# Moving a unit's y product behind the next unit's scores, in one PSUM tile of four banks

## The chip, the core and the metric

The kernel runs on one core of one Trainium2 chip. Its time is the device time of one execution in microseconds (us). Of the kernel before, three runs took 572.52, 573.49 and 574.24 us, so the median is 573.49 us. The profile shows one execution of 573.5 us, whose span from the first to the last instruction is 571.7 us. The other 1.8 us lie around the span.

## The reference

A gated linear attention is followed by two mixtures of matrix products, all in float32. For each of 32 rows (batch x head), the sequence of 768 positions is cut into chunks:

```python
L = np.exp(cum[:, :, :, None] - cum[:, :, None, :]) * causal
CB = np.einsum('bhin,bhjn->bhij', Cc, Bc)
y = np.einsum('bhij,bhjd->bhid', CB * L, xc) + np.einsum('bhin,bhnd->bhid', Cc, state) * decay_to_i
state = decay_full * state + np.sum(Bx, axis=2)
...
a = x @ w1; b = x @ w2; x = (a * b @ w3) @ w_out          # 3072 tokens, 256 -> 1024 -> 256
h = np.maximum(x @ w_in, 0.0); out = (h * h) @ w_out2       # 256 -> 2048 -> 256
```

## The kernel before, in words

The tokens are worked in eight blocks of 384 tokens (here blocks 0 to 7, so that the third block is block 2). A large product is three passes of TensorE over split operands (high x high, high x low, low x high, `mm3`, line 187), each a 128x128 by 128x384 matmul. w3 and w_out are multiplied together once, into `wc`. A block has two phases. Phase a has eight slots (m = 0 to 7): twelve matmuls for a and b into two PSUM tiles `w`, a copy on ScalarE (ACT, `asb`), a product on VectorE (DVE, `pr`), a cast on ACT (`s3h`) and a remainder on DVE (`s3l`, line 537), and three slots later six matmuls that sum x2 into two tiles `acc`. Phase h has sixteen slots (slots 8 to 23 of the block): six matmuls into a tile `w`, the relu on ACT (`r`), its square on GpSimd (POOL, `q`), the square's cast on ACT (`s3h`), the remainder on DVE (`s3l`, line 577), and three slots later six matmuls into two `acc` tiles. At the start of phase h three products h(0), h(1) and h(2) are begun together, so three tiles are open at once.

The attention is cut into 16 units; a block needs the y of two of them. A unit has these steps. Four scans on DVE make the decays (`la`, line 347). `u_lw` (DVE, line 359) ends them. `u_bt` (line 251), `u_bd` (line 365) and `u_w2` (line 376) on POOL prepare weights. `u_cb` makes four score tiles on TensorE (line 427), and `u_gain` the state sums (line 385). `u_m` multiplies scores by decays on DVE (four times, line 438), `u_state` carries the state (DVE, line 398), `u_carry` copies it into the weights of y (ACT, four copies, line 409), `u_y` makes y on TensorE (line 445), and `u_x` and `u_xl` (lines 465 and 472) write it, split, as the x of its block. A unit's loads are `la` (line 227), `xa`, and for every second unit `ct` and `bs`.

The first two blocks and units 0 to 5 run in an order written out by hand (`ORDER`). From block 2 on the order is that of the loops `ph_a` and `ph_h`, and the steps of units 6 to 15 are put into slots by the table `AT` (lines 103 to 106 and 787 to 789): unit u is worked in block u // 2 - 1, in the slots that its row names. `run_fill` calls a slot's steps before the slot's remainder on DVE, so they stand in each engine's queue ahead of it.

PSUM has eight banks: three tiles `w`, two `acc`, two `cb`, one `yu`. A unit's scores take both `cb`, one `w` and `yu`; `yu` also holds the state sums, and later y, over the place of the fourth scores.

Of the kernel before, what the change touches and what calls it, by code (L numbers as in the profile page):

```python
# [5 lines left out]
F32 = mybir.dt.float32  # L6
F32R = mybir.dt.float32r
# [15 lines left out]
HC = HG * NCH

FBS = [TB] * 8
NF = len(FBS)
F0 = [sum(FBS[:f]) for f in range(NF)]
FB = max(FBS)
M1 = FF1 // 128
M2 = FF2 // 128  # L30
KD = DM // 128
# [13 lines left out]
EARLY = 6  # L45
PLANNED = 2
# [53 lines left out]
}  # L100


AT = [
    [0, 1, 3, 5, 5, 6, 7, 7, 7, 8, 9, 9, 11, 13, 14, 14, 14],
    [6, 6, 13, 13, 14, 16, 18, 18, 19, 19, 19, 20, 20, 22, 22, 22, 23],
]


class Plan:
# [25 lines left out]
def mixer_kernel(ctx, tc, a, bct, xb, cst, *rest):  # L135
# [15 lines left out]
    nc = tc.nc  # L151
# [6 lines left out]
    at = ctx.enter_context(tc.tile_pool(name="at", bufs=2))  # L158
    sb = ctx.enter_context(tc.tile_pool(name="sb", bufs=2))
    late = ctx.enter_context(tc.tile_pool(name="late", bufs=1))  # L160
    ps_w = ctx.enter_context(tc.tile_pool(name="ps_w", bufs=3, space=PSUM))
    ps_acc = ctx.enter_context(tc.tile_pool(name="ps_acc", bufs=2, space=PSUM))
    ps_cb = ctx.enter_context(tc.tile_pool(name="ps_cb", bufs=2, space=PSUM))
    ps_yu = ctx.enter_context(tc.tile_pool(name="ps_yu", bufs=1, space=PSUM))

    cs = const.tile([TA, TB], F32, name="cs")
    sel = const.tile([128, 2 * H], F32R, name="sel")
# [13 lines left out]
    def f32(t):  # L181
        return t.bitcast(F32)
# [42 lines left out]
    def load_la(u):  # L225
        t = at.tile([TA, LA], F32, tag="la", name="la")
        nc.sync.dma_start(out=t, in_=az[u:u + 1, :].to_broadcast([TA, LA]))
        raw.setdefault(u, {})["la"] = t

    def load_xa(u):  # L230
        t = at.tile([TA, HC * D + HC * N], F32, tag="xa", name="xa")
        nc.sync.dma_start(out=t[0:T, :], in_=xb[u])  # L232
        raw.setdefault(u, {})["xa"] = t

    def load_ct(j, h):

# [141 lines left out]
    def u_gain(u):  # L378

        d = un[u]  # L380
        b = bd[u % 2]
        for c in range(NCH):
            for h in range(HG):
                i = h * NCH + c
                nc.tensor.matmul(  # L385
                    d["yu"][32 * h:32 * h + 32, TB + c * D:TB + (c + 1) * D],
                    lhsT=b[:, i * N:i * N + 2 * N],
                    rhs=d["xa"][0:T, i * D:(i + 1) * D],
                    start=True, stop=True,
                )  # L390

    def u_state(u):

        d = un[u]
        s = st[u % 2]
        c0 = NCH * ((u // 2) % 2)
        for c in range(NCH):
            nc.vector.scalar_tensor_tensor(
                s[:, c0 + c + 1, :], s[:, c0 + c, :], w2s[u % 2][:, c:c + 1],
                d["yu"][:, TB + c * D:TB + (c + 1) * D], ALU.mult, ALU.add,  # L400
            )

    def u_carry(u):

        d = un[u]
        s = st[u % 2]
        c0 = NCH * ((u // 2) % 2)
        for h in range(HG):
            nc.scalar.copy(
                d["xa"][T:TA, h * NCH * D:(h + 1) * NCH * D].rearrange("p (c d) -> p c d", d=D),  # L410
                s[32 * h:32 * h + N, c0:c0 + NCH, :],
            )

    def u_cb(u):


        d = un[u]
        hs = range(HG)
        for h in range(2):
            d["cb", h] = ps_cb.tile([128, TB], F32, tag="cb", name="cb")  # L420
        d["cb", 2] = ps_w.tile([128, 512], F32, tag="w", name="cbw")[:, 0:TB]
        d["yu"] = ps_yu.tile([128, 512], F32, tag="yu", name="yu")
        d["cb", 3] = d["yu"][:, 0:TB]
        for c in range(NCH):
            for h in hs:
                r = slice(32 * h, 32 * h + N)
                nc.tensor.matmul(  # L427
                    d["cb", h][0:TA, c * T:(c + 1) * T],
                    lhsT=bt[u % 2][r, c, :],
                    rhs=d["ct"][r, c * T:(c + 1) * T],  # L430
                    start=True, stop=True,
                )

    def u_m(u, h):

        d = un[u]
        s = d["la"][:, h * LH:h * LH + TB]
        nc.vector.tensor_tensor(s, d.pop(("cb", h))[0:TA, :], s, op=ALU.mult)

    def u_y(u):  # L440
        d = un[u]
        for c in range(NCH):
            for h in range(HG):
                i = h * NCH + c
                nc.tensor.matmul(  # L445
                    d["yu"][32 * h:32 * h + 32, c * T:(c + 1) * T],
                    lhsT=d["xa"][:, i * D:(i + 1) * D],
                    rhs=d["la"][:, h * LH + c * T:h * LH + (c + 1) * T],
                    start=True, stop=True,
                )  # L450

    def u_x(u):

        d = un[u]
        d["x"] = []
        j, g = divmod(u, 2)
        at0 = j * TB
        while at0 < (j + 1) * TB:
            f = max(f for f in range(NF) if F0[f] <= at0)
            end = min(F0[f] + FBS[f], (j + 1) * TB)  # L460
            if f not in xt:
                xt[f] = [sb.tile([128, KD, FB], F32R, tag=f"xt{p}", name=f"xt{p}", bufs=2) for p in "hl"]
            hi, lo = (t[:, g, at0 - F0[f]:end - F0[f]] for t in xt[f])
            src = d["yu"][:, at0 - j * TB:end - j * TB]
            nc.scalar.copy(hi, src)
            d["x"].append((lo, src, hi))
            at0 = end

    def u_xl(u):
        raw.pop(u)  # L470
        for lo, src, hi in un.pop(u)["x"]:
            nc.vector.tensor_tensor(lo, src, f32(hi), op=ALU.subtract)

    def u_loads(u):
        if u < NU:
            load_la(u)
            load_xa(u)
            if u % 2:
                for h in range(HG):
                    load_ct(u // 2, h)  # L480
                    load_bt(u // 2, h)

    def unit_steps(u):
        return [
            *(lambda h=h: u_decay(u, h) for h in range(HG)),
            lambda: (u_lw(u), u_bt(u)),
            lambda: (u_bd(u), u_w2(u)),
            lambda: (u_cb(u), u_gain(u)),
            lambda: u_m(u, 2),
            lambda: u_m(u, 3),  # L490
            lambda: u_state(u),
            lambda: u_m(u, 0),
            lambda: u_m(u, 1),
            lambda: u_carry(u),
            lambda: u_y(u),
            lambda: u_loads(u + 2),
            lambda: u_x(u),
            lambda: u_xl(u),
        ]

    pt = {}
    x2 = {}
    qt = {}
    acc = {}
    hp = {}
# [46 lines left out]
    def ff_h1(f, m, k, which=(0, 1, 2)):  # L552
        x = x2[f]
        if m not in hp:
            hp[m] = ps_w.tile([128, 512], F32, tag="w", name="pw")[:, 0:FBS[f]]
        mm3(hp[m], [t[:, k, m * 128:(m + 1) * 128] for t in wi], [t[:, k, :] for t in x], k == 0, k == KD - 1, which)

    hr = {}
# [217 lines left out]
    plan.run(ORDER)  # L776


    fill = {}
    at_slot = [PLANNED * (M1 + M2)]  # L780

# [2 lines left out]
            f()  # L784
        at_slot[0] += 1

    for u in range(EARLY, NU):
        for i, f in zip(AT[u % 2], unit_steps(u)):
            fill.setdefault((u // 2 - 1) * (M1 + M2) + i, []).append(f)

    def ph_a(f, tail):
        for m in range(M1):
# [111 lines left out]
```

## Time and profile before

| what | value |
|---|---|
| median of three runs | 573.49 us |
| profiled execution | 573.5 us, span 571.7 us |
| TensorE busy | 561.6 us, 98% of the span |
| weight loads busy (PEld) | 538.4 us, 94% |
| DVE, ACT, POOL busy | 330.8, 287.8, 134.7 us |
| granted TensorE clock | full in all 40 slices of the span |
| chain that ended last | TensorE 91%, DMA 6% |

A row of a timeline gives the start, the duration, the engine, the line, the operation, what it writes and reads, how many such instructions are merged, and in brackets how long the engine had been idle and what released it. Starts of successive rows tell what an engine's rate is; the duration of a matmul includes its way through the array, so it overlaps the next. For a merged row on DVE, ACT or POOL the duration runs from the first start to the last end.

### The profile page before, as it was taken

How to read it: one execution, taken by the hardware profiler on the slowest of the kernel's cores; microseconds unless marked ns; L12 is line 12 of the kernel's file. 1: busy time of each engine (PE TensorE's matmuls, PEld its weight loads, DVE VectorE, ACT ScalarE, POOL GpSimd, SP SyncE). 2: the span in 40 equal slices, each digit the busy share in tenths (PEclk: the TensorE clock that was granted, in tenths of full speed). 3: DMA queues.
4: the chain of work that ended last, by engine and by line, in shares of the span. 5: the costliest groups of instructions: out<-in, count | busy, mean ns of one | idle time of the engine just before them, and what ended most of it. 6: DMA issues, size and time to landing. Idle time of an engine off the chain costs nothing.

```text
span 571.7 us, 11523 instructions
## 1 busy us (share of the span) xinstructions
PE 561.6 (98%) x4518; PEld 538.4 (94%) x4518; DVE 330.8 (58%) x625; ACT 287.8 (50%) x611; POOL 134.7 (24%) x210
## 2 busy tenths in 40 slices
PE   8988999999999999999999999999999999999997
PEld 5866999999999999999999999999999999999997
DVE  6879899993655456435554556535554556433421
ACT  2688777853446326443455326443454326443443
POOL 3133214010000014421153014421253014410342
PEclk9999999999999999999999999999999999999999
DMA  8998967100121001040021302040022200000000
GB/s 224 385 338 277 292 197 206 50 1 29 50 58 49 29 1 57 16 97 29 1 70 57 69 2 64 8 99 28 1 70 69 59 1 1 1 2 29 0 1 28
DMA packets 17182, 43.53 MB, mean 76 GB/s; under 512 B 2744, under 2 KB 7080, under 8 KB 17128
## 3 DMA queue, kind: packets, MB, share of 16 engines
q1 hardware_dynamic: 16840, 42.58, 24.5%
q8 instruction: 35, 0.57, 0.4%
q10 hardware_dynamic: 288, 0.22, 0.2%
q14 instruction: 19, 0.16, 0.1%
HBM read 39.55 MB, written 3.25 MB: 75 GB/s over the span
## 4 chain that ended last, share of the span: by engine, by line
PE 91%; DMA 6%; SPq 1%; ACT 1%; DVE 1%; POOL 0%; issue 0%; ACTq 0%; POOLq 0%
PE pw L187 48%; PE acc L187 36%; DMA rawl<-in_w3t 3%; PE acc L616 2%; PE cb L427 2%; PE yu L445 2%; DMA rawe<-in_w3t 2%; DMA ct<-in_bct 1%; PE yu L385 1%; SPq L247 0%; ACT wch L630 0%; SPq L277 0%; DVE la L347 0%; ACT rawe L294 0%; SPq L232 0%
## 5 line engine op out<-in xcount | busy, mean ns | idle before, releaser
L577 DVE TENSOR_TENSOR s3l<-q,s3h 128x384 fp32r<-128x384 f32 x128 | 75.6, 598 | 102.9 <-POOL q L570 88.3
L187 PE MATMUL acc<-s3h,wo 128*128 128x384 f32 x512 | 132.4, 340 | 0.0
L570 POOL TENSOR_TENSOR q<-r 128x384 f32<-128x384 f32 x97 | 84.2, 870 | 185.9 <-ACT r L562 167.8
L562 ACT ACTIVATE r<-pw 128x384 f32<-128x384 f32 x128 | 62.3, 488 | 89.1 <-PE pw L187 85.5
L187 PEld LDWEIGHTS acc<-s3h,wo 128*128 128x128 f32 x512 | 91.9, 188 | 1.8
L187 PE MATMUL pw<-x2h,wih 128*128 128x384 f32 x256 | 86.6, 338 | 0.0
L187 PE MATMUL pw<-x2h,wil 128*128 128x384 f32 x256 | 86.4, 338 | 0.0
L187 PE MATMUL acc<-s3l,wo 128*128 128x384 f32 x256 | 86.1, 336 | 0.0
L187 PE MATMUL pw<-x2l,wih 128*128 128x384 f32 x256 | 84.9, 339 | 0.0
L524 DVE TENSOR_TENSOR pr<-pw,asb 128x384 f32<-128x384 f32 x64 | 35.6, 557 | 66.3 <-PE pw L187 60.3
L574 ACT ACTIVATE s3h<-r 128x384 fp32r<-128x384 f32 x128 | 67.0, 525 | 11.3 <-PE acc L187 7.7
L534 ACT CAST s3h<-pr 128x384 fp32r<-128x384 f32 x55 | 28.3, 514 | 65.4 <-DVE pr L524 61.8
L520 ACT COPY asb<-pw 128x384 f32<-128x384 f32 x64 | 30.6, 479 | 46.4 <-PE pw L187 45.4
L347 DVE TENSOR_TENSOR_SCAN la<-la,cs 112x384 f32<-112x384 f32 x48 | 49.0, 1042 | 0.0
L187 PEld LDWEIGHTS pw<-x2h,wih 128*128 128x128 f32 x256 | 48.1, 188 | 0.3
L187 PEld LDWEIGHTS acc<-s3l,wo 128*128 128x128 f32 x256 | 48.0, 188 | 0.3
L187 PEld LDWEIGHTS pw<-x2l,wih 128*128 128x128 f32 x256 | 47.9, 188 | 0.3 <-DVE x2l L550 0.3
L187 PEld LDWEIGHTS pw<-x2h,wil 128*128 128x128 f32 x256 | 48.1, 188 | 0.0
L365 POOL TENSOR_TENSOR bd<-xa,la 96x256 f32<-96x256 f32 x16 | 11.5, 720 | 142.6 <-DVE la L359 133.0
L187 PE MATMUL pw<-xth,w1h 128*128 128x384 f32 x128 | 43.6, 341 | 0.0
L187 PE MATMUL pw<-xth,w2h 128*128 128x384 f32 x128 | 43.6, 340 | 0.0
L187 PE MATMUL pw<-xth,w1l 128*128 128x384 f32 x128 | 43.3, 338 | 0.0
(109 smaller groups left out, 1040.3 us busy)
## 6 DMA issues: line engine op xcount, KB each, us to landing
la<-az SPq DMA_DIRECT2D x12, 679.0 KB, 4.6
xa<-in_xb SPq DMA_DIRECT2D x16, 288.0 KB, 5.6
rawe<-in_w3t SPq DMA_DIRECT2D x9, 512.0 KB, 9.3
rawl<-in_wo SPq DMA_DIRECT2D x7, 512.0 KB, 7.3
rawl<-in_w3t SPq DMA_DIRECT2D x7, 512.0 KB, 9.1
out_t<-o SPq DMA_DIRECT2D x16, 192.0 KB, 2.0
rawe<-in_wo SPq DMA_DIRECT2D x5, 512.0 KB, 7.6
rawl<-in_w SPq DMA_DIRECT2D x5, 512.0 KB, 9.1
```

The lines of the kernel that those rows point to most:

```text
L187: nc.tensor.matmul(ps, lhsT=w[i == 1], rhs=x[i == 2], start=first and i == 0, stop=last and i == 2)
L347: nc.vector.tensor_tensor_scan(la[:, 0:TB], src[:, 0:TB], cs, 0.0, ALU.mult, ALU.add)
L365: nc.gpsimd.tensor_tensor(bd[u % 2][:, 0:HC * N].rearrange("p (h c n) -> p h c n", h=HG, n=N), d["xa"][0:T, HC * D:].rearrange("p (h c n) ...
L427: nc.tensor.matmul(d["cb", h][0:TA, c * T:(c + 1) * T], lhsT=bt[u % 2][r, c, :], rhs=d["ct"][r, c * T:(c + 1) * T], start=True, stop=True,)
L445: nc.tensor.matmul(d["yu"][32 * h:32 * h + 32, c * T:(c + 1) * T], lhsT=d["xa"][:, i * D:(i + 1) * D], rhs=d["la"][:, h * LH + c * T:h * L ...
L520: nc.scalar.copy(ab[m], ab.pop((m, 0)))
L524: nc.vector.tensor_tensor(pr, ab.pop((m, 1)), ab[m], op=ALU.mult)
L534: (nc.scalar.copy if eng == "ACT" else on[eng].tensor_copy)(pt[f, m][0], ab[m])
L562: nc.scalar.activation(hr[m], hp.pop(m), AF.Relu)
L570: on[eng].tensor_tensor(q, hr[m], hr[m], op=ALU.mult)
L574: nc.scalar.activation(qt[f, m][0], hr[m], AF.Square)
L577: nc.vector.tensor_tensor(qt[f, m][1], hr.pop((m, 0)), f32(qt[f, m][0]), op=ALU.subtract)
```

## The change

From unit 6 on a unit's scores, state sums and the y of the unit before it are issued together (`u_turn`): scores of unit u, state sums of unit u, y of unit u - 1. They lie in one PSUM tile `ub` of four banks: bank h holds the scores of head h in columns 0 to 383, y of chunk h in the next 96, and the state sums of chunk h in 32 more. For it the pools `w`, `cb` and `yu` are closed after the first two blocks, and `w` is opened anew with two tiles. The third product of phase h takes a tile `acc` in place of a third `w`. The slots of the steps come from new tables. Units 6, 7 and 8 have slots of their own, counted from the start of block 2; from unit 9 on an odd unit's turn is in slot 8, an even one's in slot 20, and its scans 6 to 3 slots earlier. The y of unit 15 has a turn of its own.

```diff
-AT = [
-    [0, 1, 3, 5, 5, 6, 7, 7, 7, 8, 9, 9, 11, 13, 14, 14, 14],
...
+STEP_AT = {6: (0, 1, 2, 3, 3, 4, 5), 7: (9, 10, 11, 11, 12, 12, 13), 8: (14, 15, 16, 17, 18, 18, 20)}
+STEP_BY = (-6, -5, -4, -3, -3, -2, 0)
+LATER = (0, 1, 2, 2, 2, 3, 3, 4)
...
     def u_cb(u):
+            for h in range(HG):
+                d["cb", h] = ub[0][:, h, 0:TB]
+            d["g"] = [ub[0][:, c, TB + T:TB + T + D] for c in range(NCH)]
+            d["y"] = ub[0][:, :, TB:TB + T]
...
     def u_loads(u):
-        if u < NU:
+        if EARLY + 2 <= u < NU:
...
+    def u_turn(u):
+        if u < NU:
+            u_cb(u)
+            u_gain(u)
+        if u > EARLY:
+            u_y(u - 1)
...
+    def u_then(u):
+        steps = [
+            lambda: u_turn(u),
+            lambda: (u > EARLY and u_x(u - 1), u_loads(u + 1)),
+            lambda: u > EARLY and u_xl(u - 1),
+            lambda: u_state(u),
+            lambda: u_m(u, 2),
+            lambda: u_m(u, 3),
+            lambda: (u_carry(u), u_m(u, 0)),
+            lambda: u_m(u, 1),
...
     def ff_h1(f, m, k, which=(0, 1, 2)):
-            hp[m] = ps_w.tile([128, 512], F32, tag="w", name="pw")[:, 0:FBS[f]]
+            pool, tag = (ps_acc, "acc") if f >= PLANNED and m == 2 else (ps_w, "w")
+            hp[m] = pool.tile([128, 512], F32, tag=tag, name="p" + tag)[:, 0:FBS[f]]
...
+    ps_w = ctx.enter_context(tc.tile_pool(name="ps_w2", bufs=2, space=PSUM))
+    ps_u = ctx.enter_context(tc.tile_pool(name="ps_u", bufs=1, space=PSUM))
+    ub.append(ps_u.tile([128, HG, 512], F32, tag="ub", name="ub"))
...
+    for u in range(EARLY, NU + 1):
+        base = PLANNED * (M1 + M2)
+        at_u = [base + i for i in STEP_AT.get(u, ())]
+        if not at_u:
+            turn = (u // 2 - 1) * (M1 + M2) + 8 - 12 * (1 - u % 2)
+            at_u = [turn + i for i in STEP_BY]
+        if u < NU:
+            for i, f in zip(at_u, u_first(u)):
+                fill.setdefault(i, []).append(f)
+        for i, f in zip(LATER, u_then(u)):
+            fill.setdefault(at_u[-1] + i, []).append(f)
```

On TensorE, the y of a unit before the change, in block 2 between the product h (`pw`) and the output sum (`acc`) of a slot:

```order
L187 MATMUL pw<-x2h,wil 128x384
L187 MATMUL pw<-x2l,wih 128x384
L445 MATMUL yu<-la,xa 32x96 x16
L187 MATMUL acc<-s3h,wo_1426 128x384 x2
L187 MATMUL acc<-s3l,wo_1426 128x384
```

The same place of block 2 after it (the turn of unit 7, in slot 13):

```order
L185 MATMUL pw<-x2l,wih 128x384
L434 MATMUL ub<-ct,bt_104 112x96 x16
L385 MATMUL ub<-xa,bd_98 32x32 x16
L453 MATMUL ub<-la,xa 32x96 x16
L185 MATMUL acc<-s3h,wo_1063 128x384 x2
L185 MATMUL acc<-s3l,wo_1063 128x384
```

The sixteen y products no longer stand alone between large matmuls; they follow the state sums of the next unit. Nine y products (units 6 to 14) do so, that of unit 15 stands alone as before.

On ACT, the start of phase h of block 2 before (`x2h` is the last of phase a, `r` a relu, `s3h` a cast):

```order
L547 CAST x2h<-acc 128x384 x2
L562 ACTIVATE r<-pw 128x384
L574 ACTIVATE s3h<-r 128x384
L562 ACTIVATE r<-pw 128x384
L574 ACTIVATE s3h<-r 128x384
```

and after, at the same place:

```order
L557 CAST x2h<-acc 128x384 x2
L573 ACTIVATE r<-pw 128x384
L585 ACTIVATE s3h<-r 128x384
L410 COPY xa<-st_101 16x128 x4
L573 ACTIVATE r<-pw 128x384
L585 ACTIVATE s3h<-r 128x384
L573 ACTIVATE r<-pacc 128x384
```

The four copies of unit 6's state (`xa`) stand behind the first cast, ahead of the relu that empties the third product's `acc` tile.

On DVE, the start of phase h of block 2 before, from the remainders `x2l` on (the scans, `la<-la,cs`, of unit 7 stand in slot 6 and in slot 13):

```order
L550 TENSOR_TENSOR x2l<-acc,x2h 128x384 x2
L398 SCALAR_TENSOR_TENSOR st_101<-st_101,w2s_99,yu 128x32 x4
L577 TENSOR_TENSOR s3l<-q,s3h 128x384
L438 TENSOR_TENSOR la<-cb,la 112x384 x2
L577 TENSOR_TENSOR s3l<-q,s3h 128x384 x4
L347 SCALAR_TENSOR_TENSOR la<-la,cs 112x384 x2
```

and after, from the remainder of slot 7 on:

```order
L534 TENSOR_TENSOR pr<-pw,asb 128x384
L399 SCALAR_TENSOR_TENSOR st_101<-st_101,w2s_99,ub 128x32 x4
L445 TENSOR_TENSOR la<-ub,la 112x384
L547 TENSOR_TENSOR s3l<-pr,s3h 128x384
L560 TENSOR_TENSOR x2l<-acc,x2h 128x384 x2
L445 TENSOR_TENSOR la<-ub,la 112x384 x2
L588 TENSOR_TENSOR s3l<-q,s3h 128x384
L445 TENSOR_TENSOR la<-ub,la 112x384
L346 SCALAR_TENSOR_TENSOR la<-la,cs 112x384
L588 TENSOR_TENSOR s3l<-q,s3h 128x384
L346 SCALAR_TENSOR_TENSOR la<-la,cs 112x384
L588 TENSOR_TENSOR s3l<-q,s3h 128x384
```

Unit 6's state and a score product now stand ahead of the remainder of slot 7, and all four scans of unit 7 between the remainders of slots 8 to 11; two more scans, one remainder and `u_lw` follow.

## Rows read from the trace of the kernel before

**Rows 1.** Busy time by engine, one block's length: stretch, length, then each engine
```profile
251.00:315.10 64.10, 64.10 (x530) 62.49 (x529) 33.37 (x62) 28.63 (x62) 17.91 (x28) 1.00 0.17 44
```

**Rows 2.** Timeline of TensorE around the y of unit 6, block 2
```profile
223.90 0.34 PE L187 MATMUL pw<-x2l,wih 128*128 128x384 f32 x1
224.17 0.87 PE L445 MATMUL yu<-la,xa 112*32 112x96 f32 x32
224.97 0.61 PE L187 MATMUL acc<-s3h,wo 128*128 128x384 f32 x2
...
226.13 0.34 PE L187 MATMUL pw<-x2h,wih 128*128 128x384 f32 x1
```

**Rows 3.** Timeline of TensorE around unit 7's scores and state sums, block 2
```profile
235.73 0.34 PE L427 MATMUL cb<-ct,bt 16*112 16x96 f32 x2
...
236.70 0.46 PE L385 MATMUL yu<-xa,bd 96*32 96x32 f32 x32
237.09 0.62 PE L187 MATMUL acc<-s3h,wo 128*128 128x384 f32 x2
```

**Rows 4.** Instructions of line 385: shortest, median, longest ns
```profile
L385 PE MATMUL yu<-xa,bd x512: 195/196/218, 16.3 to 493.4; 96*32 96x32 f32 x171
```

**Rows 5.** Timeline of DVE in block 7, the last product of phase a
```profile
530.61 0.56 DVE L524 TENSOR_TENSOR pr<-pw,asb 128x384 f32<-128x384 f32 x1 [1.12 <-PE pw L187]
```

**Rows 6.** Timeline of TensorE there, the last pass of slot 7 into x2
```profile
532.81 0.34 PE L187 MATMUL acc<-s3l,wch 128*128 128x384 f32 x1
```

**Rows 7.** Timeline of DVE in block 2, a unit's state
```profile
238.27 1.09 DVE L398 SCALAR_TENSOR_TENSOR st<-st,w2s,yu 128x32 f32<-128x32 f32 x4
```

**Rows 8.** Timeline of TensorE, start of phase h of block 2
```profile
217.57 0.34 PE L187 MATMUL pw<-x2l,wih 128*128 128x384 f32 x1
...
220.38 0.51 PE L187 MATMUL acc<-s3h,wo 128*128 128x384 f32 x2
```

**Rows 9.** Timeline of ACT there
```profile
218.00 0.49 ACT L562 ACTIVATE r<-pw 128x384 f32<-128x384 f32 x1 [1.69 <-PE pw L187]
218.52 0.53 ACT L574 ACTIVATE s3h<-r 128x384 fp32r<-128x384 f32 x1
218.96 0.47 ACT L562 ACTIVATE r<-pw 128x384 f32<-128x384 f32 x1
...
221.88 1.25 ACT L409 COPY xa<-st 16x128 f32<-16x128 f32 x4
223.16 0.49 ACT L562 ACTIVATE r<-pw 128x384 f32<-128x384 f32 x1
```

**Rows 10.** Timeline of DVE in phase h of block 2
```profile
219.49 0.56 DVE L577 TENSOR_TENSOR s3l<-q,s3h 128x384 fp32r<-128x384 f32 x1 [1.58 <-POOL q L570]
219.96 1.01 DVE L438 TENSOR_TENSOR la<-cb,la 112x384 f32<-112x384 f32 x2
220.90 1.50 DVE L577 TENSOR_TENSOR s3l<-q,s3h 128x384 fp32r<-128x384 f32 x2
...
225.07 2.43 DVE L347 TENSOR_TENSOR_SCAN la<-la,cs 112x384 f32<-112x384 f32 x2
```

**Rows 11.** Timeline of POOL in phase h of block 2
```profile
222.07 1.01 POOL L570 TENSOR_TENSOR q<-r 128x384 f32<-128x384 f32 x1 [0.56 <-DVE s3l L577]
...
224.91 0.93 POOL L570 TENSOR_TENSOR q<-r 128x384 f32<-128x384 f32 x1 [0.35 <-ACT r L562]
...
228.78 0.51 POOL L251 COPY bt<-bs 128x384 f32<-128x384 f32 x1
...
233.01 0.62 POOL L365 TENSOR_TENSOR bd<-xa,la 96x256 f32<-96x256 f32 x1
```

**Rows 12.** DMA issues in block 2, us to landing
```profile
la<-az SPq DMA_DIRECT2D x1, 679.0 KB, 4.4
```

**Rows 13.** Timeline of DVE in block 2, the product of slot 2 of phase a
```profile
195.33 0.56 DVE L524 TENSOR_TENSOR pr<-pw,asb 128x384 f32<-128x384 f32 x1 [0.25 <-PE pw L187]
```

**Rows 14.** Timeline of TensorE there, the second product of slot 3
```profile
196.12 0.34 PE L187 MATMUL pw<-xth,w2h 128*128 128x384 f32 x1
```

More of the change, by code (lines that the diff above doesn't have):

```diff
@@ L100 @@
 }
-AT = [
-    [0, 1, 3, 5, 5, 6, 7, 7, 7, 8, 9, 9, 11, 13, 14, 14, 14],
-    [6, 6, 13, 13, 14, 16, 18, 18, 19, 19, 19, 20, 20, 22, 22, 22, 23],
-]
+STEP_AT = {6: (0, 1, 2, 3, 3, 4, 5), 7: (9, 10, 11, 11, 12, 12, 13), 8: (14, 15, 16, 17, 18, 18, 20)}
+STEP_BY = (-6, -5, -4, -3, -3, -2, 0)
+LATER = (0, 1, 2, 2, 2, 3, 3, 4)
 class Plan:
@@ L160, in mixer_kernel @@
     late = ctx.enter_context(tc.tile_pool(name="late", bufs=1))
-    ps_w = ctx.enter_context(tc.tile_pool(name="ps_w", bufs=3, space=PSUM))
     ps_acc = ctx.enter_context(tc.tile_pool(name="ps_acc", bufs=2, space=PSUM))
-    ps_cb = ctx.enter_context(tc.tile_pool(name="ps_cb", bufs=2, space=PSUM))
-    ps_yu = ctx.enter_context(tc.tile_pool(name="ps_yu", bufs=1, space=PSUM))
+    ps_early = [tc.tile_pool(name=f"ps_{k}", bufs=n, space=PSUM) for k, n in (("w", 3), ("cb", 2), ("yu", 1))]
+    ps_w, ps_cb, ps_yu = (p.__enter__() for p in ps_early)
     cs = const.tile([TA, TB], F32, name="cs")
@@ L325, in mixer_kernel @@
     xt = {}
+    ub = []
     def u_rows(u, h):
@@ L381, in u_gain @@
         b = bd[u % 2]
+        g = d.get("g") or [d["yu"][:, TB + c * D:TB + (c + 1) * D] for c in range(NCH)]
         for c in range(NCH):
@@ L385, in u_gain @@
                 nc.tensor.matmul(
-                    d["yu"][32 * h:32 * h + 32, TB + c * D:TB + (c + 1) * D],
+                    g[c][32 * h:32 * h + 32],
                     lhsT=b[:, i * N:i * N + 2 * N],
@@ L396, in u_state @@
         c0 = NCH * ((u // 2) % 2)
+        g = d.get("g") or [d["yu"][:, TB + c * D:TB + (c + 1) * D] for c in range(NCH)]
         for c in range(NCH):
@@ L399, in u_state @@
                 s[:, c0 + c + 1, :], s[:, c0 + c, :], w2s[u % 2][:, c:c + 1],
-                d["yu"][:, TB + c * D:TB + (c + 1) * D], ALU.mult, ALU.add,
+                g[c], ALU.mult, ALU.add,
             )
@@ L418, in u_cb @@
         hs = range(HG)
[L419 to L423, printed above, removed]
+        if u < EARLY:
+            for h in range(2):
+                d["cb", h] = ps_cb.tile([128, TB], F32, tag="cb", name="cb")
+            d["cb", 2] = ps_w.tile([128, 512], F32, tag="w", name="cbw")[:, 0:TB]
+            d["yu"] = ps_yu.tile([128, 512], F32, tag="yu", name="yu")
+            d["cb", 3] = d["yu"][:, 0:TB]
+        else:
+            for h in range(HG):
+                d["cb", h] = ub[0][:, h, 0:TB]
+            d["g"] = [ub[0][:, c, TB + T:TB + T + D] for c in range(NCH)]
+            d["y"] = ub[0][:, :, TB:TB + T]
         for c in range(NCH):
@@ L441, in u_y @@
         d = un[u]
+        d["y"] = d["y"] if u >= EARLY else d["yu"][:, 0:TB].rearrange("p (c i) -> p c i", i=T)
         for c in range(NCH):
@@ L445, in u_y @@
                 nc.tensor.matmul(
-                    d["yu"][32 * h:32 * h + 32, c * T:(c + 1) * T],
+                    d["y"][32 * h:32 * h + 32, c, :],
                     lhsT=d["xa"][:, i * D:(i + 1) * D],
@@ L454, in u_x @@
         d = un[u]
[L455 to L467, printed above, removed]
+        f, g = divmod(u, 2)
+        if g == 0:
+            xt[f] = [sb.tile([128, KD, FB], F32R, tag=f"xt{p}", name=f"xt{p}", bufs=2) for p in "hl"]
+        hi, lo = (t[:, g, :].rearrange("p (c i) -> p c i", i=T) for t in xt[f])
+        nc.scalar.copy(hi, d["y"])
+        d["x"] = [(lo, d["y"], hi)]
     def u_xl(u):
@@ L474, in u_loads @@
     def u_loads(u):
-        if u < NU:
+        if EARLY + 2 <= u < NU:
             load_la(u)
             load_xa(u)
-            if u % 2:
+            if u % 2 == 0:
                 for h in range(HG):
@@ L481, in u_loads, with u_first @@
                     load_bt(u // 2, h)
-    def unit_steps(u):
+    def u_turn(u):
[4 more added lines that the diff above has]
+            u_y(u - 1)
+    def u_first(u):
         return [
@@ L487, in unit_steps @@
             lambda: (u_bd(u), u_w2(u)),
-            lambda: (u_cb(u), u_gain(u)),
+        ]
+    def u_then(u):
[4 more added lines that the diff above has]
+            lambda: u_state(u),
             lambda: u_m(u, 2),
             lambda: u_m(u, 3),
-            lambda: u_state(u),
-            lambda: u_m(u, 0),
+            lambda: (u_carry(u), u_m(u, 0)),
             lambda: u_m(u, 1),
[L494 to L498, printed above, removed]
         ]
+        return steps if u < NU else steps[:3]
     pt = {}
@@ L776, in mixer_kernel @@
     plan.run(ORDER)
+    for p in reversed(ps_early):
+        p.__exit__(None, None, None)
+    ps_w = ctx.enter_context(tc.tile_pool(name="ps_w2", bufs=2, space=PSUM))
+    ps_u = ctx.enter_context(tc.tile_pool(name="ps_u", bufs=1, space=PSUM))
+    ub.append(ps_u.tile([128, HG, 512], F32, tag="ub", name="ub"))
     fill = {}
@@ L785, in run_fill @@
         at_slot[0] += 1
-    for u in range(EARLY, NU):
-        for i, f in zip(AT[u % 2], unit_steps(u)):
-            fill.setdefault((u // 2 - 1) * (M1 + M2) + i, []).append(f)
+    for u in range(EARLY, NU + 1):
[9 more added lines that the diff above has]
+            fill.setdefault(at_u[-1] + i, []).append(f)
     def ph_a(f, tail):
```

## The prediction, made before the changed kernel ran

> **What bounds the kernel now.** I read the page's busy times first, then the busy time of one steady block, then TensorE's timeline around a unit's two visits, and last the timelines of ACT, DVE and POOL at the places where the change puts new work. From block 2 on TensorE has no gap: in a block of 64.10 us it is busy 64.10 us, while DVE works 33, ACT 29 and POOL 18 us [rows 1]. Large matmuls start 0.176 us apart. So each 0.1 us that TensorE's stream loses or gains is a change of the end, and the other engines matter only where TensorE comes to wait for them. The profiled execution took 573.5 us (span 571.7 and 1.8 around it), the median of the runs; I count from it.
>
> **What goes: y standing alone.** The last large matmul before a y starts at 223.90, y at 224.17, the next large matmul at 224.97, and the one six later at 226.13 [rows 2]. That is 2.23 us in which seven starts at 0.176 would take 1.23, so a y costs 1.00: 0.09 that it starts late, 0.80 for itself, and 0.10 that the six behind it take longer. Behind the state sums the first and the last are not paid again, since the turn pays them once: 0.19. The third part is the emptying of the array: the large matmuls behind the state sums start at 237.09, when the last of these (0.20 us long, in a group that ends at 237.16) still has 0.07 to go [rows 3, 4]. If y may follow at the pitch of the state sums (0.39 over 32 is 0.01), it starts some 0.11 earlier than a large matmul could: 0.30 in all. No y of this trace stands directly behind state sums, so 0.19 and 0.30 are my bounds. I take 0.30, since both products have columns of 32 and more than 64 rows, and inside either group the starts follow one another without a gap. The Trainium skill (TensorEngine Tiling (Array Packing), Tiling Modes) says that changing the tiling mode drains the engine, and that another tile of the same mode does not. By it the pair stays in one mode, which would give 0.30; no run here shows it. Nine y products move (units 6 to 14): 9 x 0.30 = 2.7 us gained, 1.7 at the lower bound.
>
> **What comes: waits in block 2.** Block 2 has its own slots for units 6 and 7, and three places there make TensorE wait.
>
> First, slot 7. Unit 6's state and a score product now stand on DVE between the slot's product and its remainder, which the last pass into x2 needs. In block 7, where nothing is in between, this pass starts 2.20 after the product [rows 5, 6]. Now the remainder starts after the product's 0.47 (the pitch of such products), the state's 1.0 (four instructions in 1.09 [rows 7]) and another 0.47, and ends 0.56 later, at 2.5: a wait of 0.3. Before, the slot's scores gave TensorE 1.5 us of other work there, and they now stand two slots earlier.
>
> Second, slot 8. The second output sum of a block takes the `acc` tile that the third product h(2) borrowed, so it waits for the third relu. Let P be the start of the last matmul of h(0), 217.57 here; the second output sum then starts at P + 2.81 [rows 8]. On ACT the first relu starts at P + 0.43, the cast 0.52 later; then come the four copies of the state, 1.28 until the next instruction, then the second relu, its cast (0.52 on) and the third relu (0.44 on, 0.47 long) [rows 9]. Sum: 0.43 + 0.52 + 0.53 + 1.28 + 0.52 + 0.44 + 0.47 = 4.2. TensorE waits 1.4, and everything behind is late by it. Without the copies the third relu would end at about P + 2.8, with no wait.
>
> Third, the turn of unit 7 in slot 13. Its state sums need `bd`, which needs `u_lw`, which stands on DVE behind all four scans and the remainder of slot 11. After the second wait the last matmul of slot 13's h starts 20 starts behind P + 4.2, at P + 7.7; the scores come 0.27 later [rows 2], the state sums 0.97 after those [rows 3]: P + 9.0. On DVE the remainder of slot 8 starts at P + 1.92 and the first scan two pitches of 0.47 later, P + 2.9 [rows 10]. From there scans, remainders and POOL's squares go one after another, because they block one another. The square that began at 224.91 ended at 225.84, and the scan issued at 225.07 beside it pushed the pair's end to 227.50: 2.43 us, where two scans take 1.66 from the square's end on [rows 10, 11]. In the other direction, the square issued at 222.07 beside a remainder that ended at 222.40 took 1.01 [rows 10, 11]. Score products, which read PSUM, run freely beside squares: two took 1.01 [rows 10]. The Trainium skill (SBUF — State Buffer, Who interferes with whom) says that a DVE instruction with two SBUF inputs and a GpSimd instruction that reads SBUF exclude one another for a whole instruction. The trace agrees, with the 0.93 and 2.43 above, and the rule speaks against putting scans beside the squares. The sum: four scans at 0.83 (half of 1.66), 3.3; three remainders at 0.47, 1.4; `u_lw` about 0.1; four squares, at 0.68 (what the blocked one took after 222.40) to 0.83, 2.7 to 3.3; `bt` 0.5 and `bd` 0.6 [rows 11]: 8.6 to 9.2, so `bd` is ready at P + 11.5 to 12.1. TensorE waits 2.5 to 3.1; I take 2.8. If DVE and POOL did not block one another, `bd` would be ready near P + 9.2, a wait of 0.2; that is the lower bound.
>
> **What comes elsewhere.** In blocks 3 to 6 the odd unit's turn in slot 8 gives ACT over 2 us before the second relu, but `u_x` of slot 9 (a cast, 0.44 to 0.5 of ACT) stands ahead of the third. Counted from the second relu, the third ends 0.52 + 0.44 + 0.46 + 0.47 = 1.89 later, and the output sum's place is 1.85 later: 0.05 each, 0.2 together. If ACT's instructions went end to start it would be 0.3 each, 1.2 together. Block 7 has no unit: nothing, at most 0.3. In phase a two tiles `w` in place of three: the product of slot 2 ends at 195.89 and its tile is wanted at 196.12 [rows 13, 14], so 0.2 is left; nothing, at most 0.1 in each of six blocks and 0.1 in each of three slots of block 2. Unit 8's `la` is loaded in slot 14, behind unit 6's y, and its first scan stands in the same slot. The load takes 4.4 [rows 12], in which DVE stands; remainders are needed three slots (6.3) later, and by the sums above DVE has 0.5 to 1.4 to spare in slots 18 to 20: nothing, at most 1.5. The later even units' scans share slots 14 to 17 with squares, but have 2.8 us to spare before their turn. Reading y across four banks, the merged loads and the moved copies lie beside TensorE's work. Before, y of an odd unit was split in slot 23; now this is done by slot 22, so the block's change is safer than it was.
>
> **The sum:** 573.5 - 2.7 + 0.3 + 1.4 + 2.8 + 0.2 = 575.5 us, 0.35% slower. All bounds to one side give 570.8 and 579.9.
>
> **Rivals.** (A) The change pays what it costs: scans and squares do not hold each other up as I read from single rows, and unit 7's `bd` comes almost in time. Then 0.2 stands for 2.8: 572.9. For it: only one scan of this trace was seen blocked in each block, and who gets the port next is not visible. Against: both directions show it.
>
> (B) No new wait reaches TensorE in block 2: the third relu is early enough, or the sum's tile is not the borrowed one, and POOL prepares unit 7 in time. Then only the merging is left, 573.5 - 2.7 + 0.2 = 571.0, faster. For it: in the old order TensorE waits nowhere from block 2 on. Against: the copies stand on ACT ahead of that relu, and the second output sum has a wait for ACT of its own.
>
> (C) Slower still: DVE does not recover from unit 8's load. It decides from the point at which `la` lands 0.5 to 1.4 us later than the 4.4 shown, or scans in slots 14 to 17 meet a square each (4 x 0.7 = 2.8 us more of DVE's time against that spare). Then the remainders of slots 15 and 16, and unit 8's `bd`, come late, for 1.5 to 2 us: 577.3.
>
> **Chances.** Forecast 0.46, A 0.25, B 0.17, C 0.12. A run of this kernel can tell 0.3%, 1.7 us, from no change: faster is below 571.8, slower above 575.2. The forecast's own range is 574 to 577, two thirds of it slower; with C this makes 0.44 slower. B and a little of A are faster, 0.20. The rest, 0.36, is the same. The range runs from B's middle to C's middle, 571.1 to 577.4.
>
> **What would show it.** In the profile after: y starts within 0.05 us of the last state sum, and the stretch from the last large matmul before a turn to the seventh behind it is some 2.25 us above seven starts, where the two visits cost 2.54. In block 2 TensorE is idle 0.3 before the last pass into x2 (remainder on DVE), 1.4 before the second output sum (ACT's relu), 2.8 before unit 7's state sums (POOL's `bd`); scans in slots 9 to 11 are longer than 1.4 us where a square runs. Blocks 3 to 6 are shorter than 64.1 by 0.5. I am wrong if block 2 shows no idle time on TensorE, if blocks 3 to 6 are not shorter, or if TensorE waits in each block for a tile `w`.

## The result

The changed kernel took 578.98 us (median of four runs, 577.73 to 579.44), the kernel before 573.87 us in the same comparison. The ratio is 1.0087, 95% interval [1.0059, 1.0114]: slower by 3.4 to 6.5 us. The prediction said 575.5 us, at most 577.4. The sign was right, the size was not, and the time lies outside the range.

The profiled execution took 579.13 us, its span 577.3 us, 5.6 more than before. A span can be cut where the same work begins in both kernels: at the first product of block 2, and at the second cast `x2h` of each block on ACT. In us:

| stretch | before | after | difference |
|---|---|---|---|
| ahead of block 2 | 188.72 | 190.30 | +1.58 |
| phase a of block 2 | 27.11 | 27.56 | +0.45 |
| from there to the same place of block 3 | 64.10 | 69.21 | +5.11 |
| three more such stretches, each | 64.10 | 63.60 | -0.50 |
| the stretch into block 7 | 62.54 | 62.34 | -0.20 |
| the rest | 36.93 | 37.09 | +0.16 |
| from the start of block 2 to the end | 382.98 | 387.00 | +4.02 |

Ahead of block 2 both kernels give every engine the same instructions in the same order, and in the traces of the experiments below, which share them, this point lies between 187.28 and 188.77. So I do not count the 1.58 us as the change's. One part of them shows in the traces: after the change the granted clock was at its lower level from 47.2 to 50.6 us, before it was not; where the rest comes from is not shown. What belongs to the change in this execution is 4.02 us.

### The profile page after: what moved, and what is told of

It reads as the page before. It is cut to its first block, busy times and chain, and to the rows that moved or that the text cites. A ratio compares the mean times of both kernels' runs of the same rounds, so it can differ in the third digit from the quotient of the medians.

```text
span 577.3 us, 11494 instructions
## 1 busy us (share of the span) xinstructions
PE 563.5 (98%) x4518; PEld 540.8 (94%) x4518; DVE 333.7 (58%) x625; ACT 288.6 (50%) x611; POOL 143.9 (25%) x210
## 4 chain that ended last, share of the span: by engine, by line
PE 87%; DMA 6%; DVE 4%; ACT 1%; issue 1%; POOL 1%; SPq 0%; DVEq 0%; ACTq 0%; POOLq 0%
PE pw L185 45%; PE acc L185 33%; DMA rawe<-in_w3t 3%; PE acc L627 2%; PE ub L434 2%; DMA rawl<-in_w3t 2%; PE ub L453 1%; DMA rawl<-in_wo 1%; PE pacc L185 1%; PE ub L385 1%; DVE la L346 1%; PE cb L434 1%; PE yu L453 1%; DVE v L305 1%; DVE st L399 0%
## 5 line engine op out<-in xcount | busy, mean ns | idle before, releaser
L588 DVE TENSOR_TENSOR s3l<-q,s3h 128x384 fp32r<-128x384 f32 x128 | 78.2, 619 | 104.5 <-POOL q L581 71.1
L581 POOL TENSOR_TENSOR q<-r 128x384 f32<-128x384 f32 x97 | 90.7, 937 | 188.3 <-ACT r L573 181.3
L573 ACT ACTIVATE r<-pw 128x384 f32<-128x384 f32 x122 | 59.5, 489 | 103.7 <-PE pw L185 100.7
L185 PE MATMUL pw<-x2h,wih 128*128 128x384 f32 x244 | 83.0, 340 | 0.0
L185 PE MATMUL pw<-x2h,wil 128*128 128x384 f32 x244 | 82.4, 338 | 0.0
L185 PE MATMUL pw<-x2l,wih 128*128 128x384 f32 x244 | 81.9, 339 | 0.1
L185 PEld LDWEIGHTS pw<-x2h,wih 128*128 128x128 f32 x244 | 45.9, 188 | 0.9
L185 PEld LDWEIGHTS pw<-x2l,wih 128*128 128x128 f32 x244 | 45.7, 188 | 0.4 <-DVE x2l L560 0.4
L185 PEld LDWEIGHTS pw<-x2h,wil 128*128 128x128 f32 x244 | 45.8, 188 | 0.0
```

Of the source, the lines that this page charges most:

```text
L185: nc.tensor.matmul(ps, lhsT=w[i == 1], rhs=x[i == 2], start=first and i == 0, stop=last and i == 2)
L573: nc.scalar.activation(hr[m], hp.pop(m), AF.Relu)
L581: on[eng].tensor_tensor(q, hr[m], hr[m], op=ALU.mult)
L588: nc.vector.tensor_tensor(qt[f, m][1], hr.pop((m, 0)), f32(qt[f, m][0]), op=ALU.subtract)
```

## The profile after

First TensorE's waits from block 2 on: the line that waited, the line waited for, us in total, times, longest. The kernel before has no such line there.

```profile
PE ub L434 <- POOL bt L249: 2.6, 1, 2.6
PE acc L185 <- ACT r L573: 1.2, 1, 1.2
PE acc L185 <- DVE s3l L547: 0.2, 1, 0.2
```

These are three waits at the three places of the forecast; the longest stands ahead of the scores, for `bt`, where the forecast had the state sums and `bd`. Then the steady blocks, by the view of [rows 1]: 63.60 us in place of 64.10, again without a gap.

```profile
287.07:350.67 63.60, 63.60 (x530) 62.51 (x529) 33.97 (x62) 28.79 (x62) 18.47 (x28) 1.00 0.18 45
```

A steady turn on TensorE's timeline, which answers to [rows 2, 3]:

```profile
312.26 0.34 PE L185 MATMUL pw<-x2l,wih 128*128 128x384 f32 x1
312.53 1.04 PE L434 MATMUL ub<-ct,bt 16*112 16x96 f32 x32
313.50 0.46 PE L385 MATMUL ub<-xa,bd 96*32 96x32 f32 x32
313.77 0.89 PE L453 MATMUL ub<-la,xa 112*32 112x96 f32 x32
314.59 0.62 PE L185 MATMUL acc<-s3h,wo 128*128 128x384 f32 x2
...
315.74 0.34 PE L185 MATMUL pw<-x2h,wih 128*128 128x384 f32 x1
```

Behind state sums y starts 0.27 after their first one, where before the large matmul started 0.39 after it. From the last large matmul ahead of the turn to the seventh behind it pass 3.48 us. Seven starts at 0.176 are 1.23, so a turn costs 2.25 where the two visits cost 2.54.

Now the turn of unit 7 in block 2, the same rows where `bd` and `bt` came late (in brackets the idle time ahead and what ended it):

```profile
227.46 0.34 PE L185 MATMUL pw<-x2l,wih 128*128 128x384 f32 x1
230.35 1.04 PE L434 MATMUL ub<-ct,bt 16*112 16x96 f32 x32 [2.55 <-POOL bt L249]
231.34 0.55 PE L385 MATMUL ub<-xa,bd 96*32 96x32 f32 x32
231.67 1.50 PE L453 MATMUL ub<-la,xa 112*32 112x96 f32 x32
233.10 1.01 PE L185 MATMUL acc<-s3h,wo 128*128 128x384 f32 x2
...
235.09 0.34 PE L185 MATMUL pw<-x2h,wih 128*128 128x384 f32 x1
```

Here 7.63 us pass in place of 3.48, 4.15 more. The scores start 2.89 behind the last large matmul, where 0.27 is the rule: 2.62 of it is the wait. The other 1.53 come behind the wait: y takes 1.50 in place of 0.89, two large matmuls 1.01 in place of 0.62. The windows view of TensorE says why (stretch, length, busy time, then the granted clock):

```profile
226.00:228.00 2.00, 1.80 (x11) 1.00 0.00 0
228.00:230.00 2.00, 0.00 (x0) 1.00 0.00 0
230.00:232.00 2.00, 1.65 (x75) 0.89 0.00 0
232.00:234.00 2.00, 2.00 (x35) 0.50 0.05 8
234.00:236.00 2.00, 2.00 (x11) 0.76 0.91 273
```

TensorE was busy up to 227.8, stood still to 230.35, and its granted clock then went from 2.4 to 1.2 GHz until about 235. The wait of 1.24 us in slot 8 has no such tail.

The work that made the turn late is on DVE and POOL, and answers to [rows 10, 11]. First DVE, then POOL:

```profile
222.47 0.95 DVE L346 TENSOR_TENSOR_SCAN la<-la,cs 112x384 f32<-112x384 f32 x1
...
226.48 3.01 DVE L346 TENSOR_TENSOR_SCAN la<-la,cs 112x384 f32<-112x384 f32 x2
229.41 0.53 DVE L588 TENSOR_TENSOR s3l<-q,s3h 128x384 fp32r<-128x384 f32 x1
229.86 0.48 DVE L358 TENSOR_TENSOR la<-la 112x16 f32<-112x16 f32 x1
```
```profile
225.38 3.29 POOL L581 TENSOR_TENSOR q<-r 128x384 f32<-128x384 f32 x2 [0.56 <-ACT s3h L585]
228.62 1.68 POOL L249 COPY bt<-bs 128x384 f32<-128x384 f32 x1
230.47 0.81 POOL L364 TENSOR_TENSOR bd<-xa,la 96x256 f32<-96x256 f32 x1 [0.17 <-issue]
```

Two scans beside squares took 3.01 us, two squares 3.29, and even the copy `bt` 1.68, where it takes 0.51 in [rows 11].

## The experiments

My theory: the change is worth nine merged y, and all it lost are the waits of block 2 and the clock behind the long one. The rivals: the clock fell for another reason (the 96 small products in one run), the waits are not where I put them, or the merged turns and the two `w` tiles have a price of their own. Every kernel below is the changed one with the edit shown, or an earlier one of these where the text or the diff says so. Times from the start of block 2 to the end (387.00 after the change, 382.98 before) come from the traces.

**Unit 6's copies later.**

```diff
-LATER = (0, 1, 2, 2, 2, 3, 3, 4)
+LATER = (0, 1, 2, 2, 2, 3, 3, 3, 4)
+LATER_6 = (0, 1, 2, 2, 2, 3, 6, 3, 4)
...
-            lambda: (u_carry(u), u_m(u, 0)),
+            lambda: u_carry(u),
+            lambda: u_m(u, 0),
```

`LATER_6` takes the place of `LATER` for unit 6 alone; the other units keep their slots. Its seventh number puts the copies six slots behind the turn in slot 5.

> Unit 6's four copies on ACT stand in slot 11 in place of slot 8. My theory (the serial work of DVE and POOL sets the turn of unit 7): the wait of 1.24 us before block 2's second output sum goes, but the turn's wait of 2.55 grows to about 3.3, since only the second square and remainder, held by the same copies, come earlier (0.65 us); the granted clock still falls behind it. So 0.6 us less than the changed kernel: ratio to before 1.006 to 1.009. Rival (each wait is a cost by itself): 1.4 us less, turn's wait 2.55 as it was.

Measured: 576.08 us, ratio 1.0053 [1.0033, 1.0072], just below the range that I gave; from block 2 on 386.33. The waits:

```profile
PE ub L435 <- POOL bt L250: 3.4, 1, 3.4
PE acc L186 <- DVE s3l L549: 0.2, 1, 0.2
```

The wait for the relu is gone, the turn's wait grew to 3.39, and the trace gained 0.67 us, as my theory had it, and not the 1.4 of the rival. One wait had covered part of the other: taking away the first of two on a path gives back only what the second does not take.

**Unit 7's scans in phase a.**

The edit is one entry of `STEP_AT`; the rest of its line is left out here and below.

```diff
-... 7: (9, 10, 11, 11, 12, 12, 13) ...
+... 7: (4, 5, 6, 6, 6, 6, 13) ...
```

> Unit 7's scans, lw, bt, bd and w2 stand in slots 4 to 6 of phase a of block 2, where POOL has no squares; its turn stays in slot 13. My theory (scans between squares, and a clock that falls because TensorE stood still): the turn takes 3.48 us from its last large matmul to the seventh behind it, as in the steady blocks, in place of 7.63; the granted clock stays full there; the wait of 1.2 us at slot 8 stays. 4.1 us less than the changed kernel, ratio to before 0.999 to 1.002. Rival on the clock (it falls because of the 96 small products in a row, or by itself): the clock falls at the turn without a wait, 1.3 us stay. Rival on the wait (bd late for another reason, as xa's or bt's data): the wait stays.

Measured: 574.28 us, ratio 1.0017 [1.0004, 1.0031], from block 2 on 385.22. The turn has neither wait nor slow clock:

```profile
224.90 0.34 PE L185 MATMUL pw<-x2l,wih 128*128 128x384 f32 x1
225.17 1.04 PE L434 MATMUL ub<-ct,bt 16*112 16x96 f32 x32
...
228.41 0.34 PE L185 MATMUL pw<-x2h,wih 128*128 128x384 f32 x1
```

3.51 us in place of 7.63: the same 96 products in a row, at full clock. So the 96 products alone do not lower the clock, and without the long wait it stays full. The ratio came out as expected, but the trace gained 1.78 us, not 4.1, since new waits stand behind:

```profile
PE acc L185 <- DVE s3l L588: 1.0, 2, 0.9
PE ub L434 <- POOL bt L249: 0.6, 1, 0.6
```

Both belong to unit 8. Its scans stand on DVE until `la` lands, and its `bt` and `bd` come late behind them. This is rival C of the prediction. In the changed kernel DVE stood 4.22 us for that load too, without a wait of TensorE. The difference is the load itself. Its DMA issue in the changed kernel, and here (the last number is the us from issue to landing):

```profile
la<-az SPq DMA_DIRECT2D x1, 679.0 KB, 4.6
```
```profile
la<-az SPq DMA_DIRECT2D x1, 679.0 KB, 7.6
```

The load is issued behind the y in unit 7's turn. So a late turn makes it late too, and does not hide it: from the last y product to unit 8's first scan pass 5.10 us in the changed kernel and 7.99 here.

**Both edits, and unit 6's state behind slot 7's remainder.** The first kernel (e3) has both edits above. The second (e4) has also this:

```diff
-LATER_6 = (0, 1, 2, 2, 2, 3, 6, 3, 4)
+LATER_6 = (0, 1, 2, 3, 3, 4, 6, 5, 6)
```

> Both edits. My theory: no wait in slot 8 and none at the turn, only the 0.46 us of slot 7 left: 5.5 us less than the changed kernel, ratio to before 0.996 to 0.999, some 572 us. Rival (the merged turns or the two w tiles cost something of their own that the waits hid): 574 or more.

> As the last, and unit 6's state and its first score product stand in slot 8, behind the remainder of slot 7. My theory: no wait on TensorE from block 2 on; 0.45 us less than the last, ratio to before 0.9945 to 0.998, some 571.3 us: what nine merged y give (2.7 us), less 0.1 for each of four blocks. Rival: the same as the last or slower, since the remainders of x2 now come behind the state.

Measured: 573.34 us, ratio 1.0002 [0.9988, 1.0015], and 571.61 us, ratio 0.9979 [0.9964, 0.9993]; from block 2 on 382.87 and 383.09. The first misses what I expected, because unit 8's waits were not in it. The second lies in the range that I gave, but not for my reason, since TensorE still waits. In its trace phase a of block 2 takes 27.11 us as before the change, so the 0.45 of slot 7 is won back, and as much and more is lost behind it: unit 8's `la` took 6.6 us to land in the first trace and 7.2 in the second. There the first scan waited for it, and TensorE for a remainder behind the scans and for `bt`:

```profile
232.88 0.96 DVE L347 TENSOR_TENSOR_SCAN la<-la,cs 112x384 f32<-112x384 f32 x1 [7.16 <-DMA la<-az]
```
```profile
PE acc L186 <- DVE s3l L590: 0.9, 1, 0.9
PE ub L435 <- POOL bt L250: 0.6, 1, 0.6
```

**Unit 8 in time, first try.**

Against the second of these:

```diff
-LATER_6 = (0, 1, 2, 3, 3, 4, 6, 5, 6)
+LATER_6 = (0, 1, 2, 3, 3, 3, 5, 4, 5)
-... 7: (4, 5, 6, 6, 6, 6, 13), 8: (14, 15, 16, 17, 18, 18, 20)}
+... 7: (4, 5, 6, 6, 6, 6, 11), 8: (15, 15, 16, 17, 17, 18, 20)}
```

> As the last, and unit 7's turn in slot 11 in place of 13 (unit 6's steps after its turn close up, its copies in slot 10), so that unit 8's la is issued two slots earlier, in slot 12; unit 8's scans begin in slot 15 in place of 14. My theory: what the last kernel still lost were the waits for unit 8 (0.86 us for a remainder held by scans that stood until la landed, 0.57 us for bt); both go, no wait on TensorE from block 2 on: 1.4 us less than the last, ratio to before 0.994 to 0.9965; from the start of block 2 to the end 2.3 us less than before. Rival (these waits come from two-input work of DVE beside squares, wherever unit 8's scans stand): at least 0.6 us of them stays.

Measured: 576.46 us, ratio 1.0073 [1.0059, 1.0087]: a miss. Unit 8's waits are gone, though its `la` took 7.6 us to land, but one that I made stands in their place:

```profile
PE ub L435 <- DVE la L446: 2.5, 1, 2.5
```

The turn in slot 11 writes the four banks, and unit 6's last score product, in slot 10 of DVE's queue behind a remainder that waits for its square, had not read its bank. With one tile for all scores a unit's turn cannot pass the last product of the unit before it. The clock fell again (0.67 as a mean over 222 to 226 us), and the wait with its tail cost 4 us: the stretch from block 2 to block 3 took 67.69 us, where the version with all waits taken away (below) takes 63.68. The profiled execution took 574.25 us, the shortest of five. The other four, 576.01 to 577.10 us, have a mean granted clock of 0.987 to 0.990 where it has 0.993, so the tail that a trace shows is that of one execution.

**The price of the merging.** On top of the first try for unit 8, y(u-1) is taken out of the turn and stands alone in the slot behind it; PSUM and the wait stay.

```diff
-        if u > EARLY:
-            u_y(u - 1)
...
-            lambda: (u > EARLY and u_x(u - 1), u_loads(u + 1)),
+            lambda: u > EARLY and (u_y(u - 1), u_x(u - 1), u_loads(u + 1)),
```

> As e5, but y(u-1) stands alone between large matmuls in the slot behind unit u's turn. Same PSUM tile, same waits. My price of the merging: 0.30 us for each of nine y products: 2.7 us more than e5, about before's time (ratio 0.9985 to 1.002). By the lower bound 0.19: 1.7 more. Rival (merging gives nothing of its own): as e5.

Measured: 579.03 us, ratio 1.0108 [1.009, 1.0126]. From block 2 on 387.52 against 385.00, 2.52 us more for nine y: 0.28 each. Steady stretches take 64.16 against 63.59.

**Squares on DVE.** As the kernel with unit 6's copies in slot 11, and:

```diff
-            h_sq(f, m)
+            h_sq(f, m, "DVE" if f == PLANNED and m < 5 else "POOL")
```

> As e1 (unit 6's copies in slot 11), but the squares of slots 8 to 12 of block 2 are made on DVE in place of POOL. My theory (a scan and a square shut one another out, so both together cost DVE the sum): on DVE a square costs 0.47 where the shut-out cost 0.7 to 0.9, and bt and bd run without a square or scan in their way: bd ready 1.2 us or more earlier, the wait at unit 7's turn falls from 3.4 to 1 to 2.2 us, in all 1 to 3.5 us less than e1. Rival (scans and squares run side by side; DVE is just full): four or five squares more on DVE, 0.47 each, make the wait about 2 us longer, 5.3, and the kernel 2 us slower than e1.

Measured: 577.72 us, ratio 1.0092 [1.0072, 1.0111] against 1.0053 [1.0033, 1.0072] without the edit, from block 2 on 386.45 against 386.33. Neither expected wait came: TensorE waited 3.06 us, now between the scores and the state sums, for `bd`. DVE's rows with the squares on DVE, then on POOL:

```profile
221.81 0.95 DVE L347 TENSOR_TENSOR_SCAN la<-la,cs 112x384 f32<-112x384 f32 x1
...
223.59 0.95 DVE L347 TENSOR_TENSOR_SCAN la<-la,cs 112x384 f32<-112x384 f32 x1
...
225.38 1.80 DVE L347 TENSOR_TENSOR_SCAN la<-la,cs 112x384 f32<-112x384 f32 x2
```
```profile
220.94 1.12 DVE L347 TENSOR_TENSOR_SCAN la<-la,cs 112x384 f32<-112x384 f32 x1
...
222.43 1.58 DVE L347 TENSOR_TENSOR_SCAN la<-la,cs 112x384 f32<-112x384 f32 x1
...
224.38 3.01 DVE L347 TENSOR_TENSOR_SCAN la<-la,cs 112x384 f32<-112x384 f32 x2
```

Four scans take 3.70 us without squares on POOL and 5.71 beside them, so scans and squares do hold one another up. But that cost DVE 2.0 us, not the 2.7 to 3.3 of my four squares, and five squares at 0.47 on DVE cost 2.35. Moving them costs DVE about what it saves.

**TensorE made to stand.** As the first try for unit 8, and in block 7 the remainder of three slots is made many times over:

```diff
+            for _ in range({2: 10, 7: 12, 12: 14}.get(m, 0) if f == NF - 1 else 0):
+                nc.vector.tensor_tensor(qt[f, m][1], hr[m, 0], f32(qt[f, m][0]), op=ALU.subtract)
             h_lo(f, m)
```

> As e5, and in block 7, where no unit is worked, the remainders of the third, eighth and thirteenth slot of phase h are made 11, 13 and 15 times over (the same values), so that TensorE stands still in front of large matmuls three times, for about 0.9, 1.9 and 2.8 us by the pitch of 0.47. My theory on the clock (it falls after a wait of 2.5 us, and not after one of 1.2, whatever comes next): full after the first, at its lower level for some 3 us after the third; the second tells on which side 1.9 lies. Rival (it fell because small products followed the wait): full after all three. Time: 5.6 us of waits and some 1.5 to 3 us of clock above e5.

Measured: 593.22 us (one run). A repeat took 0.64 us in place of 0.47, so the waits came out at 4.17, 3.05 and 4.33 us and none was short: the run could not say what a short wait does. The first, on the timeline and in the windows of TensorE (the clock behind the busy time):

```profile
549.59 0.69 PE L186 MATMUL acc<-s3l,wo 128*128 128x384 f32 x1 [4.17 <-DVE s3l L590]
```
```profile
546.00:549.00 3.00, 0.00 (x0) 0.93 0.00 0
549.00:552.00 3.00, 2.41 (x7) 0.50 0.00 0
```

Large matmuls alone stand around this wait, and the clock fell while TensorE still stood. Together with the full clock at unit 7's turn once its scans stand in phase a (above), that rules out the rival that small products lower it.

**All waits taken away.** Against the first try for unit 8:

```diff
-LATER_6 = (0, 1, 2, 3, 3, 3, 5, 4, 5)
+LATER_6 = (0, 1, 2, 3, 3, 3, 5, 4, 4)
-... 7: (4, 5, 6, 6, 6, 6, 11) ...
+... 7: (4, 5, 6, 6, 6, 6, 12) ...
```

> As e5, but unit 7's turn in slot 12, and unit 6's last score products in slot 9, so that they have read their banks before the turn writes them (e5's wait of 2.52 us was for the one in slot 10). My theory (the change is worth nine merged y less 0.06 to 0.14 us in five blocks, and all else of its time was waits in block 2 and the clock behind them): no wait in block 2, clock full there; its stretches as the steady ones, 63.7 us in place of 67.7; from the start of block 2 to the end 381.1 us (before 382.98); ratio to before 0.9945 to 0.998. Rival (the three turns of block 2 cost something besides waits): 382 or more, ratio 0.999 to 1.002.

Measured: 570.37 us, ratio 0.9955 [0.9941, 0.9969]: faster than both kernels. From block 2 on 381.01 us, the stretch from block 2 to block 3 63.68, and no wait on TensorE from block 2 on. The clock is full in all windows of block 2; the one around unit 7's turn:

```profile
222.00:226.00 4.00, 4.00 (x108) 1.00 0.17 49
```

Unit 8's `la` landed in 4.5 us here, so this trace does not tell by itself what the later scans of unit 8 are worth against a late load.

**Short stands.** On top of that, with repeats as above but fewer (7 in the fifth and 9 in the eleventh slot of block 7's phase h).

> As e9, but in block 7 the remainders of the fifth and the eleventh slot of phase h are made 8 and 10 times over; by e8 (0.64 us each; 13 gave a wait of 3.05) TensorE should stand still about 0 to 0.6 and 1.1 to 1.8 us. Theory (a short stand costs its own time and 0.1, a long one also the clock): full clock behind both if they stay near 1.3, as at slot 8 of the changed kernel; if the second comes to 1.8 it tells whether that is long. Rival (any stand lowers the clock by its length): the clock falls for about as long as each wait.

Measured: 572.49 us (one run), waits of 0.51 and 1.33 us, clock full in block 7:

```profile
544.86 0.45 PE L186 MATMUL acc<-s3l,wo 128*128 128x384 f32 x1 [0.51 <-DVE s3l L590]
559.12 0.45 PE L186 MATMUL acc<-s3l,wo 128*128 128x384 f32 x1 [1.33 <-DVE s3l L590]
```
```profile
558.00:560.00 2.00, 0.88 (x5) 1.00 0.00 0
560.00:562.00 2.00, 2.00 (x13) 1.00 0.00 0
```

The rest behind block 7's start took 39.48 us in place of 37.08, 2.4 for 1.84 of idle time. So each wait costs some 0.3 more than the idle time that the view prints: 0.17 since the view counts from the end of the last matmul, 0.34 behind its start, and the next would have started 0.176 behind it; the other 0.1 is the restart.

## Why the prediction was wrong

**The merging (2.7 us gained): right.** 0.28 for each y by the experiment, 2.5 in all. The trace bears out that y follows state sums without a new start.

**Slot 7 (0.3): right in its cause, 0.15 too small.** The view prints 0.18 of idle time, but the stretch is 0.45 longer: the last start before the wait and the first behind it are 0.53 apart, 0.35 more than the rule, and the next start is late by another 0.1. I had left out the second, the restart.

**Slot 8 (1.4): right.** The second output sum starts 1.58 behind the last matmul ahead of it, 1.40 more than 0.176. It waits for the relu, and the wait goes when the copies go.

**The turn of unit 7 (2.8): this step failed, by what follows the wait.** The wait itself was 2.62, for the serial work of scans, remainders and squares as I had added it up: from the first scan (222.47) to the end of `u_lw` (230.34) pass 7.87 us, where the sum has 7.5 to 8.1. Not as in the sum, `bt` ended it (1.68 us where I had 0.5, but beside `u_lw`, not behind it), with `bd` just behind. The step priced it at its own length. The granted clock fell to 1.2 GHz behind it and cost 1.53 more, and I had no term for that: the trace of before holds no wait of TensorE from block 2 on, and I took that as a full clock whatever happens. From block 2 on the experiments show the clock falling at every wait of 2.5 us or more, and staying full without one.

**Blocks 3 to 6 (0.5 shorter each): right.** 0.50 in three stretches, and the wait of the output sum there is 0.06, where I had 0.05. **Block 7 (nothing, at most 0.3): 0.16**, the same wait for the relu of the borrowed tile, without a turn ahead of it.

**Unit 8 (nothing, rival C at 0.12): right, with a load that landed in 4.6 us.** Where it took 6.6 to 7.6 us with the scans in the same slots, rival C's mechanism was there, and cost 1.4 to 2.4 us of the stretch from block 2 to block 3. No run has these slots without the wait ahead of them and with a short landing, so whether they would do then is not shown.

The sum by what was measured, from block 2 on: merged y -2.5, slot 7 +0.45, slot 8 +1.40, the turn +2.62 and +1.53, and the waits in blocks 3 to 7 with the restart in block 2 some +0.5: 4.0, as the trace has it. That is 0.7% of the time and inside the interval of the ratio. The forecast had 2.0, and 1.5 of the missing 2.0 are the clock. The medians are 5.1 apart, and where the other 1.1 lie is open: three of the four runs have no trace, only mean granted clocks of 0.988, 0.991 and 0.996 beside the 0.993 of the profiled one.

Two sums of the prediction are off, and neither decides: all its bounds to the slow side add up to some 580.5 us, not 579.9, and without blocking `bd` comes at P + 8.8 by its own terms, not P + 9.2.

Rival A had the turn in time, B no wait at all. Neither is the changed kernel, but the version with all waits removed took 570.37 us, so B's estimate of 571.0 was near for it. The merging pays; the slots chosen for units 6 to 8 cost more than it gave.

## What to carry to other kernels

When an engine that never stood still is made to wait, price the wait with its tail: the time to restart, and the clock. Before crediting the removal of a wait, look for the next late thing behind it, since a wait can hide a shorter one on the same path. Where a table sets the order, check each moved step against the queue of its engine, not only against the step that needs it: here DVE's place in the queue of a slot lay one to two slots of time behind TensorE's.

## What the runs showed of the hardware

From block 2 on the granted clock stayed full behind TensorE's waits of 0.51, 1.24, 1.25 and 1.33 us, and fell to its lower level at all nine waits of 2.52 to 4.33 us; none between was tried. Behind the wait of 2.55 it was low for some 3.4 us, and behind a wait of 2.52 for 3.4 in two traces and 6.8 in a third (that of "TensorE made to stand").

The length of one wait does not decide alone. Ahead of block 2, where TensorE works with more gaps, the clock fell behind a wait of 1.08 us in the trace after the change, and stayed full behind one of 1.41 at the same place in that of "The price of the merging". The end of the wait and a window behind it, first after the change:

```profile
45.77 2.76 PE L627 MATMUL acc<-wo1v,ve 128*128 128x256 f32 x8 [1.08 <-DVE wcl L645]
48.00:50.00 2.00, 1.77 (x5) 0.50 0.32 88
```
```profile
44.10 2.17 PE L627 MATMUL acc<-wo1v,ve 128*128 128x256 f32 x8 [1.41 <-DVE wcl L645]
46.00:48.00 2.00, 1.25 (x6) 1.00 0.58 174
```

So these runs give no safe length for a wait; what else decides is not shown.

Behind a wait the second large matmul starts 0.28 to 0.29 us after the first (at 545 and 559 us of the last trace), where 0.176 is the rule: a restart costs 0.1 even when the wait is short.

Unit 8's `la` load took 4.4 to 5.1 us to land in most traces, and 6.6, 7.2, 7.6 and 7.6 in four [rows 12 and the experiments]: a first scan placed in the slot of its load's issue has no margin for that.
